# Input 0's load split anew between the instruction rings and the casting ring, and dummy matmuls counted from when TensorE wakes

## The chip, the cores and the metric

The kernel runs on one core of one Trainium2 chip. The metric is device time in microseconds (us), the median of several runs. Before the change it was 435.29 us (435.23 to 435.62, 4 runs). Engine names follow the profile: PE is TensorE, PEld its weight loads, DVE is VectorE, ACT is ScalarE, POOL is GpSimd, SP is SyncE. "The casting ring" is the DMA queue that POOL feeds; in this kernel it turns fp32 into fp16 on the way. "The instruction rings" are the queues that SP and ACT feed; in this kernel they copy without a cast. In the traces, each group of input 0 that comes by them has a cast of its own on ACT or DVE (0.43 to 0.62 us each, L456), and the groups of the casting ring have none.

## The reference, cut to what matters

For each of 8 batches: a real Fourier transform along 2496 rows, a complex 256 x 256 mix with bias and soft threshold, the inverse transform, and then a mixture-of-experts layer in which each batch goes through one expert.

```
X = rfft(x, axis=1)                        # x: (8, 2496, 256) fp32
Yr = Xr @ w_r - Xi @ w_i + b_r             # and Yi alike
Y = soft_threshold(Yr) + 1j * soft_threshold(Yi)
y = irfft(Y)
e = argmax(mean(y, axis=1) @ w_gate)       # one expert per batch
out = gate * (relu(y @ w1[e]) @ w2[e])
```

Nothing can start before input 0 (batch 0 of x) is in SBUF. It has 11 column groups of 117 partitions x 512 values. The first DFT (L657) turns them into spectra, the mix (L701) multiplies by the weights, a second DFT with the tables `tf` and `tm` (L734, L737) finishes the transform, and VectorE adds the bias (z, L749) and thresholds (L762, L764). Then come the inverse (L576, L615, L1000) and the experts (L1302, L1339). The first DFT of batch 1 (L657 again, from input 1) is done between the inverse products of batch 0.

## The kernel before: the parts that matter

A list scheduler written in Python fixes the order of every engine's instructions when the kernel is built. It keeps a clock of its own: `free[e]` is the time at which engine e is assumed free, and `S.fixed(t)` is an assumed landing time of a load. These numbers only decide the order; when things run is read from the traces (in the changed kernel the copy of a table part assumed at 16.4 us runs when the part comes, at 18.81). Dummy matmuls fill assumed idle time of PE, to keep its clock up: with dummies in an early wait they come 0.22 us apart after 11 us (e8 below), without them 0.43 (e1). "Cold", "half speed" and a clock that "rises" are read from the spacings of matmuls.

```python
def run(self):
    free = dict.fromkeys(("PE", "ACT", "DVE", "SP", "POOL"), 1.3)
    free["ACT"], free["SP"], free["POOL"] = 4.0, 3.5, 6.0
    ...
XF = 4                                   # groups 0..3: instruction rings, fp32
X0_CUTS = ((4, 8), (8, 11))              # groups 4..10: casting ring, fp16
...
x0_part(nc.sync, 0, 0, 2, xf); x0_part(nc.scalar, 2, 0, 2, xf); ...
x0_part(nc.scalar, 2, 2, 4, xf); x0_part(nc.sync, 0, 2, 4, xf); ...
for c0, c1 in X0_CUTS:
    for j in (0, 2, 1):
        x0_part(nc.gpsimd, j, c0, c1, xin0)
...
X0_AT, X1_AT = (5.0, 9.0, 11.5), 27.0    # assumed landings: input 0, input 1
W_AT, T_AT = 12.9, (13.8, 16.8, 19.0)    # weights; three parts of the tables
WARM, COLD, WARM_END = 60, 10, 13.2
...
for i in range(WARM):                    # dummies; a cold one is taken as 0.43 us
    o = S.op("PE", 0.43 if i < COLD else 0.216, dummy, 1e6 + i)
    o.until = WARM_END
...
def tm_part(k0, k9, t):                  # VectorE: tm is tf with halves swapped, one negated
    ...
    return S.op("DVE", 0.1 + 0.055 * (k9 - k0), emit, -39, deps=[S.fixed(t)])
...
def load_w(_):                           # a tiny copy on POOL waits for a casting cut
    nc.gpsimd.tensor_copy(out=wf[0:1, :, 0, 0:1], in_=xin0[0:1, 4:6, 0:1])
    ...                                  # then SP loads w_r, w_i
def load_tables(_):                      # SP, behind the weights: tf, bias2, ti, in three parts
    ...
def load_1(_):                           # input 1, held behind tf's second part
    xin_t[1] = load_now(1, (0, NG // 2), tf[96:97, 11, 0:2])
```

So a chain of loads hangs together: a casting cut of input 0 lands, POOL makes a tiny copy (1 x 2 elements), SP issues weights and tables one after another, the second part of `tf` lands, POOL makes another tiny copy, and input 1 is issued on the casting ring. In the schedules below, "the gate" is the first of these copies.

Of the kernel before, what the change touches and what calls it, by code (L numbers as in the profile page):

```python
# [135 lines left out]
class Schedule:  # L136
# [59 lines left out]

    def run(self):
        free = dict.fromkeys(("PE", "ACT", "DVE", "SP", "POOL"), 1.3)
        free["ACT"], free["SP"], free["POOL"] = 4.0, 3.5, 6.0
        ring = {"SP": 19.0, "POOL": 25.5}  # L200
        todo = sorted(self.ops, key=lambda o: o.vt)
        self.log = []
        while any(not o.until for o in todo):
            best = None
            seen = {e: 0 for e in free}
            for o in todo:
                if all(seen[e] > 24 for e in o.engs):
                    continue
                r = self.ready(o)
                if r is None or (o.until and max(r, free["PE"]) > o.until):  # L210
                    continue
                for e in o.engs:
                    seen[e] += 1
                    s = max(r, free[e])
                    p = o.bias if s < RAMP else 0.0
                    if e == "DVE" and len(o.engs) > 1:
                        p += o.pen
                    if o.until:
                        p += IDLE
                    k = (s + p, o.vt, s + p + o.lat[e])  # L220
                    if best is None or k < best[0]:
                        best = (k, s, o, e)
            _, s, o, e = best
            todo.remove(o)
            for k in o.allocs:
                if k.tag in self.rings:
                    self.bank[k.tag] = self.rings[k.tag].take(k)
                else:
                    self.hist.setdefault(k.tag, []).append(k)
            free[e] = s + o.occ[e]  # L230
            o.done = s + o.lat[e]
            if o.dma:
                other = "POOL" if e == "SP" else "SP"
                t = max(ring[e], s + 1.3)
                behind = max(0.0, ring[other] - t)
                if e == "SP":
                    ext = min(2.3 * o.dma, behind)
                    ring[other] += ext / 2.3
                else:
                    ext = min(0.43 * o.dma, behind)  # L240
                    ring[other] += min(2.3 * behind, o.dma)
                ring[e] = t + o.dma + ext
                o.done = ring[e] + o.slack
            self.log.append((s, e, o))
            o.emit(e)
# [3 lines left out]
def kernel(  # L249
# [12 lines left out]
    nc = tc.nc  # L262
# [9 lines left out]
        return ctx.enter_context(tc.tile_pool(name=name, bufs=bufs, **kw))  # L272

    XROW = 2 * D + 16
    XF = 4
    X0_CUTS = ((4, 8), (8, 11))
    BUFS = {"XT": 2, "hs": 2, "z": 3, "V": 3, "Pt": 2}
    cpool = pool("consts", 1)
    xpool = pool("xp", 2)
# [18 lines left out]
    def load_now(b, cuts, hold=None):  # L298

        xin = xpool.tile([117, NG // 2, XROW], FP16, name="xin")  # L300
        if hold is not None:
            nc.gpsimd.tensor_copy(out=xin[96:97, 0, 0:2], in_=hold)
        xv = x[b].rearrange("(a n) c -> a n c", n=N2)
        for c0, c1 in zip(cuts, cuts[1:]):
            for j in range(3):
                nc.gpsimd.dma_start(
                    out=xin[39 * j : 39 * j + 39, c0:c1, 0 : 2 * D],
                    in_=xv[:, 21 * j + 2 * c0 : 21 * j + 2 * c1, :].rearrange(
                        "a (g i) c -> a g (i c)", i=2))
        return xin  # L310
# [5 lines left out]
    xin0 = xpool.tile([117, NG // 2, XROW], FP16, name="xin")  # L316
    xf = hpool.tile([117, XF, 2 * D], FP32, name="hs")
    xv = x[0].rearrange("(a n) c -> a n c", n=N2)

    def x0_part(eng, j, c0, c1, dst):  # L320
        eng.dma_start(
            out=dst[39 * j : 39 * j + 39, c0:c1, 0 : 2 * D],
            in_=xv[:, 21 * j + 2 * c0 : 21 * j + 2 * c1, :].rearrange(
                "a (g i) c -> a g (i c)", i=2))
# [2 lines left out]
    x0_part(nc.scalar, 2, 0, 2, xf)  # L327
    x0_part(nc.sync, 1, 0, 2, xf)
    nc.scalar.dma_start(out=wa, in_=d_wa.ap())
    x0_part(nc.scalar, 2, 2, 4, xf)  # L330
    x0_part(nc.sync, 0, 2, 4, xf)
    x0_part(nc.sync, 1, 2, 4, xf)
    for c0, c1 in X0_CUTS:
        for j in (0, 2, 1):
            x0_part(nc.gpsimd, j, c0, c1, xin0)
# [8 lines left out]
    for e in range(E):  # L344
        nc.vector.memset(iot[:, e : e + 1], float(E - e))
    wf = ypool.tile([P, N], FP32, name="ysb")[:, 0 : 4 * D].rearrange(
        "p (w t c) -> p w t c", w=2, t=2)
# [12 lines left out]
    KT = ((0, 4), (4, 12), (12, 20))  # L360
# [4 lines left out]
    wg16 = cpool.tile([P, 2, E], FP16, name="wg16")  # L365


    X0_AT, X1_AT = (5.0, 9.0, 11.5), 27.0
    W_AT, T_AT = 12.9, (13.8, 16.8, 19.0)



    S = Schedule(BANKS)
# [3 lines left out]
    DIRECT = 2  # L377
    WIDE1 = 1
    W_LATE = 46.0
    WARM, COLD, WARM_END = 60, 10, 13.2  # L380
    LATE = -0.12
    FAST = {(B - 1, c) for c in range(4)}
    PERIOD, SPAN, SHIFT = 49.5, 1.4, 0.6
# [18 lines left out]
    def tm_part(k0, k9, t):  # L402
        def emit(_):
            nc.vector.tensor_scalar_mul(out=tm[:, k0:k9, 0:64],
                                        in0=tf[:, k0:k9, 64:P], scalar1=-1.0)
            nc.vector.tensor_copy(out=tm[:, k0:k9, 64:P], in_=tf[:, k0:k9, 0:64])
        return S.op("DVE", 0.1 + 0.055 * (k9 - k0), emit, -39, deps=[S.fixed(t)])

    tm_in = {k: o for (k0, k9), t in zip(KT, T_AT)
             for o in [tm_part(k0, k9, t)] for k in range(k0, k9)}  # L410

    def w_products(_):
# [9 lines left out]
        for i, bv in enumerate((b_r, b_i)):  # L422
            nc.sync.dma_start(out=bias[:, i], in_=spread(bv, P))
    S.op("SP", 0.8, bias_load, W_LATE, deps=[S.fixed(W_LATE)])
    b_in = S.fixed(T_AT[0])
    yk = S.tok("ysb", 2)
    yk.rel.append(w_late)
    S.preset(yk)
# [3 lines left out]
        nc.sync.dma_start(out=wi0, in_=d_wi0.ap())  # L432
        nc.sync.dma_start(out=wi, in_=d_wi.ap())
    S.op("SP", 1.8, small_loads, -30, deps=[S.fixed(13.0)], lat=8.0)
    small = S.fixed(18.0)


    pw = ps[:, BASE["o"]]
    for i in range(WARM):
        def dummy(_):  # L440
            nc.tensor.matmul(pw, warm[:, 0:P], warm)  # L441
        o = S.op("PE", 0.43 if i < COLD else 0.216, dummy, 1e6 + i)
        o.until = WARM_END

    def wg_cast(eng):
        COPY[eng](out=wg16, in_=wg)
    wg_in = S.evac(20, wg_cast, 0.5, deps=[small])
    t_in = [S.fixed(T_AT[0 if k1 < 4 else 1 if k1 < 12 else 2])
            for k1 in range(NK1)]
    first_V2 = S.tok("V2", 2)  # L450
    S.preset(first_V2)
# [2 lines left out]
    def x_cast(c):  # L454
        def emit(eng):
            COPY[eng](out=xin0[:, c, 0 : 2 * D], in_=xf[:, c])  # L456
        return S.evac(500, emit, -60 + c, deps=[S.fixed(X0_AT[0] + 0.3 * c)])

    x_cast_ops = [x_cast(c) for c in range(XF)]
    c1, c2 = ([S.fixed(t)] for t in X0_AT[1:])  # L460
    xdone = {0: [x_cast_ops[0:2], x_cast_ops[2:4], c1, c1, c2, c2],
             1: [S.fixed(X1_AT)]}
    xin_t[0] = xin0

    def load_w(_):
        nc.gpsimd.tensor_copy(out=wf[0:1, :, 0, 0:1], in_=xin0[0:1, 4:6, 0:1])
        for i, w in enumerate((w_r, w_i)):
            nc.sync.dma_start(out=wf[:, i], in_=w.rearrange("(t p) c -> p t c", p=P))
    S.op("SP", 1.0, load_w, -80, deps=[S.fixed(7.0)])

    def load_tables(_):
# [11 lines left out]

    def load_1(_):
        xin_t[1] = load_now(1, (0, NG // 2), tf[96:97, 11, 0:2])
    S.op("POOL", 2.4, load_1, -78, deps=[S.fixed(14.5)])
    xtok = {b: S.tok("xin", 2) for b in range(B)}
    for b in range(2):
        S.preset(xtok[b])
# [947 lines left out]
```

## Time and profile before

| | before |
|---|---|
| time | 435.29 us |
| span of the profiled run | 434.1 us |
| PE wakes / first real matmul (L657) | 3.87 / 8.96 us |
| gate (POOL) | 9.67 us |
| mix (L701) starts | 16.78 us |
| second z on DVE (L749) | 20.84 us |
| first DFT of batch 1 | 32.34 us |
| first expert matmul (L1302) | 47.64 us |

The page of the kernel before gives the span, then the busy time of each engine with its share, and, in part 4, the chain of work that ended last.

```profile
span 434.1 us, 9428 instructions
PE 423.7 (98%) x3572; PEld 314.9 (73%) x3572; DVE 301.9 (70%) x616; ACT 332.7 (77%) x643; POOL 33.1 (8%) x54
PE 93%; DVE 3%; ACT 2%; issue 1%; ACTq 0%
```

PE bounds the kernel, but "busy" includes the dummies. The timeline of PE before shows them. The columns are start, duration, engine, line, operation, output<-input, size, how many in a row, and in brackets the idle time before and what ended it.

```profile
3.87 5.30 PE L441 MATMUL ps<-warm 128*128 128x512 f16 x12 [3.87 <-ACT warm L339]
8.96 1.53 PE L657 MATMUL ps<-wa,xin 117*128 117x120 f16 x16
10.33 2.11 PE L441 MATMUL ps<-warm 128*128 128x512 f16 x9
12.28 1.00 PE L657 MATMUL ps<-wa,xin 117*128 117x120 f16 x16
13.12 1.68 PE L441 MATMUL ps<-warm 128*128 128x512 f16 x7
14.63 0.73 PE L657 MATMUL ps<-wa,xin 117*128 117x120 f16 x12
15.21 1.46 PE L441 MATMUL ps<-warm 128*128 128x512 f16 x6
...
32.34 0.58 PE L657 MATMUL ps<-wa,xin 117*128 117x120 f16 x8
...
47.64 1.02 PE L1302 MATMUL ps<-ysb,w1s 128*128 128x512 f16 x4
```

No L657 up to 16 us has a bracket: PE never waits for data, its data waits behind dummies. PE wakes 2.6 us later than the 1.3 us that the scheduler assumed, so every dummy is that late.

### The profile page before, as it was taken

The page shows a single profiled execution, that of the slowest core. Times are in us where ns is not written, and L with a number is a line of the kernel's source. Part 1 is how long each engine was busy: PE and PEld are TensorE (multiplying, and loading weights), DVE is VectorE, ACT ScalarE, POOL GpSimd, SP SyncE. Part 2 cuts the span into 40 slices and gives each one's busy share as a digit, 9 for nine tenths or more (in the row PEclk, how much of TensorE's full clock was granted, in tenths as well). Part 3 has the DMA queues.
Part 4 walks back from the last instruction along what each step waited for, and adds up shares of the span by engine and source line. Part 5 has one row for each costly group of instructions (what it writes and reads, how often), then busy time and mean ns, then how long its engine had stood idle before and what let it go on. Part 6 is the DMA issues. An engine that isn't in the chain of part 4 may idle for free.

```text
span 434.1 us, 9428 instructions
## 1 busy us (share of the span) xinstructions
PE 423.7 (98%) x3572; PEld 314.9 (73%) x3572; DVE 301.9 (70%) x616; ACT 332.7 (77%) x643; POOL 33.1 (8%) x54
## 2 busy tenths in 40 slices
PE   6998999999999999999999999999999999999996
PEld 3557666778777877778677777778777787777775
DVE  1488866577967687786977878777877869513661
ACT  3589987688877787678867888768777788678884
POOL 3230100021002000021001100020000010000000
PEclk9999999999999999999999999999999999999999
DMA  8899197989994998879986998959977276522122
GB/s 166 223 160 171 33 228 227 215 160 189 231 277 121 226 188 227 241 151 217 189 236 206 189 204 207 292 96 233 207 211 227 101 140 148 173 91 74 50 99 92
DMA packets 85605, 77.20 MB, mean 178 GB/s; under 512 B 7610, under 2 KB 72398, under 8 KB 85560
## 3 DMA queue, kind: packets, MB, share of 16 engines
q1 hardware_dynamic: 68366, 57.73, 47.7%
q0 software_dynamic: 16880, 18.46, 27.7%
q8 instruction: 28, 0.46, 0.4%
q10 hardware_dynamic: 314, 0.41, 0.3%
q14 instruction: 17, 0.14, 0.1%
HBM read 57.54 MB, written 37.49 MB: 219 GB/s over the span
## 4 chain that ended last, share of the span: by engine, by line
PE 93%; DVE 3%; ACT 2%; issue 1%; ACTq 0%
PE ps L1302 31%; PE ps L1339 29%; PE ps L897 9%; PE ps L1042 4%; PE ps L529 4%; PE ps L795 3%; PE ps L859 3%; PE ps L701 3%; PE ps L1221 2%; PE ps L441 2%; DVE z L749 1%; PE ps L734 1%; PE ps L657 1%; PE ps L737 1%; DVE Y L764 1%
## 5 line engine op out<-in xcount | busy, mean ns | idle before, releaser
L1314 ACT ACTIVATE hs<-ps 128x512 f16<-128x512 f32 (+1 forms) x293 | 168.2, 594 | 68.1 <-PE ps L1302 64.3
L1302 PE MATMUL ps<-ysb,w1s 128*128 128x512 f16 (+1 forms) x640 | 178.2, 374 | 0.0
L1339 PE MATMUL ps<-w2s,hs 128*128 128x256 f16 x1152 | 162.3, 272 | 0.1
L1339 PEld LDWEIGHTS <-hs 128*128 128x128 f16 x1152 | 110.8, 98 | 42.7 <-issue 0.2
L1302 PEld LDWEIGHTS <-w1s 128*128 128x128 f16 x640 | 68.6, 113 | 18.6 <-issue 0.2
L911 DVE TENSOR_TENSOR tt<-ps,bias 128x512 f16<-128x512 f32 x60 | 38.6, 686 | 24.5 <-PE ps L897 24.5
L939 DVE TENSOR_TENSOR Y<-z,cl 64x512 f16<-64x512 f16 x120 | 50.4, 420 | 2.8
L897 PE MATMUL ps<-w,XT 128*128 128x256 f16 x360 | 49.4, 273 | 0.0
L1356 ACT ACTIVATE ost<-ps,gbc 128x512 f32<-128x512 f32 x65 | 44.8, 689 | 2.3 <-PE ps L1339 2.3
L897 PEld LDWEIGHTS <-XT 128*128 128x128 f16 x360 | 35.2, 98 | 7.7
L920 DVE TENSOR_TENSOR z<-ps,tt 128x512 f16<-128x512 f32 x60 | 38.4, 681 | 0.1
L805 ACT CAST A<-ps 120x512 f16<-120x512 f32 x48 | 29.4, 613 | 7.2 <-PE ps L795 6.8
L1058 DVE CAST ysb<-ps 128x468 f16<-128x468 f32 (+1 forms) x24 | 15.0, 630 | 25.6 <-PE ps L1042 25.5
L1058 ACT CAST ysb<-ps 128x468 f16<-128x468 f32 (+1 forms) x60 | 28.0, 522 | 3.2 <-PE ps L1042 2.6
L867 DVE CAST XT<-ps 128x512 f16<-128x512 f32 x24 | 16.5, 688 | 16.0 <-PE ps L859 16.0
L536 ACT CAST V<-ps 128x512 f16<-128x512 f32 x45 | 26.1, 607 | 0.0
L795 PE MATMUL ps<-xin,wa 117*120 117x512 f16 x66 | 23.1, 380 | 0.4 <-ACT ysb L1015 0.4
L1042 PE MATMUL ps<-wi,V 120*128 120x117 f16 (+1 forms) x308 | 22.4, 214 | 0.0
L867 ACT CAST XT<-ps 128x512 f16<-128x512 f32 x36 | 22.0, 614 | 0.0
L529 PE MATMUL ps<-Y,ti 128*128 128x256 f16 x140 | 21.8, 272 | 0.0
L536 DVE CAST V<-ps 128x512 f16<-128x512 f32 x25 | 17.2, 688 | 6.4 <-PE ps L529 5.4
L1042 PEld LDWEIGHTS <-V 120*128 120x128 f16 x308 | 19.8, 98 | 2.4
(104 smaller groups left out, 421.6 us busy)
## 6 DMA issues: line engine op xcount, KB each, us to landing
out_dram<-ost SPq DMA_DIRECT2D x72, 256.0 KB
xin<-in_x_dram POOLq DMA_DIRECT2D x21, 429.0 KB, 11.0
scr<-V SPq DMA_DIRECT2D x35, 256.0 KB
XB<-fwd SPq DMA_DIRECT2D x30, 256.0 KB
V<-scr SPq DMA_DIRECT2D x14, 504.0 KB
fwd<-A SPq DMA_DIRECT2D x18, 360.0 KB
w1s<-in_moe_w_dram POOLq DMA_DIRECT2D x8, 512.0 KB, 7.3
w2s<-in_moe_w_dram POOLq DMA_DIRECT2D x8, 512.0 KB, 8.8
```

The source lines that it names most:

```text
L529: nc.tensor.matmul(pv[:, D * i : D * i + D], ti[:, 4 * q + k, :], cell["Y"](k))
L536: COPY[eng](out=hc["V"][:, n * u : n * u + n].rearrange("p i c -> p (i c)"), in_=hc["p", u])
L867: COPY[eng](out=cell["X"][:, ch, :, 0:2].rearrange("p a r i k -> p a i r k"), in_=hc["p"].rearrange("p (a i r k) -> p a i r k", a=2, i=2, ...
L897: nc.tensor.matmul(pm[:, D * a : D * a + D], cell["X"][:, ch, a, t].rearrange("p i k -> p (i k)"), w4[:, ch, t, :], start=(ch == 0), stop= ...
L911: nc.vector.tensor_add(out=cell["tt"][:, r], in0=cell["T", 2].rearrange("p (a c) -> p a c", a=2), in1=bias[:, r].unsqueeze(1).to_broadcast ...
L939: nc.vector.tensor_sub(out=Y[64 * r : 64 * r + 64, :, i], in0=cell["z"][s, r], in1=cell["cl"][s, r])
L1042: nc.tensor.matmul(pi[:, 117 * i : 117 * i + M], V2[:, g, ch * P : ch * P + P], w)
L1058: COPY[eng](out=yv[:, :, 12 * gb : 12 * gb + 3 * nf].rearrange("p a (g j) -> p a g j", j=3), in_=pi[:, 0 : 117 * nf].rearrange("p (g a j) ...
L1302: nc.tensor.matmul(ph[:, 0:nl], w1v[:, ch, fc // 4, :, fc % 4], ysb_t[b][:, ch, ns : ns + nl], start=(ch == 0), stop=(ch == 1))
L1314: nc.scalar.activation(out=o, in_=i, func=AFT.Relu)
L1339: nc.tensor.matmul(oc["p"][:, i, :], cell["hs"][:, ft, s0 : s0 + P], w2s_t[b][:, ft, :], start=(ft == 0), stop=(ft == E - 1))
L1356: nc.scalar.activation(out=ost, in_=oc["p"], func=AFT.Copy, scale=gbc_t[b])
```

## The change

Its intent is to start the real work as early as the data allows. Only groups 0 and 1 stay on the instruction rings. The casting ring takes nine groups in three cuts. PE's dummies are counted from 3.85 us, and the assumed landings are all moved earlier to suit.

```diff
-        free["ACT"], free["SP"], free["POOL"] = 4.0, 3.5, 6.0
-        ring = {"SP": 19.0, "POOL": 25.5}
+        free["PE"], free["ACT"], free["SP"], free["POOL"] = 3.85, 4.0, 3.5, 6.0
+        ring = {"SP": 17.5, "POOL": 26.0}
@@
-    XF = 4
-    X0_CUTS = ((4, 8), (8, 11))
+    XF = 2
+    X0_CUTS = ((2, 6), (6, 9), (9, 11))
@@
-    x0_part(nc.scalar, 2, 2, 4, xf)
-    x0_part(nc.sync, 0, 2, 4, xf)
-    x0_part(nc.sync, 1, 2, 4, xf)
@@
-    X0_AT, X1_AT = (5.0, 9.0, 11.5), 27.0
-    W_AT, T_AT = 12.9, (13.8, 16.8, 19.0)
+    X0_AT, X1_AT = (5.2, 7.6, 9.4, 10.8), 26.5
+    W_AT = 11.6
+    TF_AT, TI_AT = (12.3, 14.4, 16.4), (13.2, 15.4, 17.4)
@@
-    WARM, COLD, WARM_END = 60, 10, 13.2
+    WARM, COLD, WARM_END = 60, 12, 11.9
@@ (load_w's gate now reads the second of the three cuts)
-        nc.gpsimd.tensor_copy(out=wf[0:1, :, 0, 0:1], in_=xin0[0:1, 4:6, 0:1])
+        nc.gpsimd.tensor_copy(out=wf[0:1, :, 0, 0:1], in_=xin0[0:1, 6:8, 0:1])
... (the uses of these constants, and smaller assumed times, cut)
```

Lines of the changed kernel are two below those of before: L657 becomes L655, L701 becomes L699, L749 becomes L747, L1302 becomes L1300. Experiments on the kernel before keep its lines; in e10 and e11 the lines after the table loads are one below those of before (L749 becomes L748).

More of the change, by code (lines that the diff above doesn't have):

```diff
@@ L407, in tm_part @@
         return S.op("DVE", 0.1 + 0.055 * (k9 - k0), emit, -39, deps=[S.fixed(t)])
-    tm_in = {k: o for (k0, k9), t in zip(KT, T_AT)
+    tm_in = {k: o for (k0, k9), t in zip(KT, TF_AT)
              for o in [tm_part(k0, k9, t)] for k in range(k0, k9)}
@@ L424 @@
     S.op("SP", 0.8, bias_load, W_LATE, deps=[S.fixed(W_LATE)])
-    b_in = S.fixed(T_AT[0])
+    b_in = S.fixed(13.0)
     yk = S.tok("ysb", 2)
@@ L434 @@
     S.op("SP", 1.8, small_loads, -30, deps=[S.fixed(13.0)], lat=8.0)
-    small = S.fixed(18.0)
+    small = S.fixed(16.5)
     pw = ps[:, BASE["o"]]
@@ L447 @@
     wg_in = S.evac(20, wg_cast, 0.5, deps=[small])
-    t_in = [S.fixed(T_AT[0 if k1 < 4 else 1 if k1 < 12 else 2])
+    t_in = [S.fixed(TI_AT[0 if k1 < 4 else 1 if k1 < 12 else 2])
             for k1 in range(NK1)]
@@ L456, in emit @@
             COPY[eng](out=xin0[:, c, 0 : 2 * D], in_=xf[:, c])
-        return S.evac(500, emit, -60 + c, deps=[S.fixed(X0_AT[0] + 0.3 * c)])
+        return S.evac(500, emit, -60 + c, deps=[S.fixed(X0_AT[0])])
     x_cast_ops = [x_cast(c) for c in range(XF)]
-    c1, c2 = ([S.fixed(t)] for t in X0_AT[1:])
-    xdone = {0: [x_cast_ops[0:2], x_cast_ops[2:4], c1, c1, c2, c2],
+    c1, c2, c3 = ([S.fixed(t)] for t in X0_AT[1:])
+    xdone = {0: [x_cast_ops, c1, c1, c2, c3, c3],
              1: [S.fixed(X1_AT)]}
@@ L485, in load_1 @@
         xin_t[1] = load_now(1, (0, NG // 2), tf[96:97, 11, 0:2])
-    S.op("POOL", 2.4, load_1, -78, deps=[S.fixed(14.5)])
+    S.op("POOL", 2.4, load_1, -78, deps=[S.fixed(13.5)])
     xtok = {b: S.tok("xin", 2) for b in range(B)}
```

## The prediction

> **What bounds the kernel.** The page shows TensorE (PE) busy 98% of a 434.1 us span and holding 93% of the chain that ended last; the table of stretches shows it at 100% from 50 to 400 us. So time saved before the first expert matmul (L1302, 47.6 us) can reach the end one for one; the rest of the program changes only in order.
>
> **The start, from the timeline.** PE wakes at 3.87 us, but the schedule counts dummies from 1.3 us, so it emits twelve cold ones of 427 ns (3.87 to about 9.0). The first two column groups were cast by 6.4 us (casts 5.23 to 6.37), yet the first DFT matmul (L657) starts at 8.96, behind dummies. It repeats: nine dummies from 10.33, seven from 13.12, six from 15.21. PE never waits for a load here; its queue is about 2.6 us late. The chain runs dummies, L657, dummies, L657, dummies, L657, weight cast, then L701 at 16.78.
>
> **Loads.** Groups 2 and 3 on the instruction rings landed only at 9.33 us. The DMA view gives about 8.2 us from issue to landing for the casting transfers, so the first cut landed between 9.7 and 11.3 us, the second at 12 to 13. The DMA engines are 96% busy or more from 4 to 10 us, so moving two groups to another ring removes no work, only competition: [...] the casting queue moved 386 packets in 5 to 8 us beside the instruction rings, 497 in 8 to 10 us alone. From those rates I estimate that the three new cuts land near 7.8, 9.6 and 11.2 us. Weight loads now wait for the first part of the second cut, near 8.4 us instead of 9.67; the tables behind them come 1 to 1.5 us earlier.
>
> **What changes.** Two casts of 0.43 to 0.62 us go. POOL issues nine transfers of 0.63 us instead of six, until about 7.2 us; off the chain. About five dummies precede the first L657, near 6.0 us. The last L657 group starts near 11.2 instead of 14.6, its eviction (0.96 us) ends near 12.6, weights are cast by 12.4, and L701 starts near 13.0 instead of 16.78.
>
> **What reaches the end.** 3.7 us is freed at L701. Tables and input 1 come only 1 to 2 us earlier (input 1 landed near 30 us, first used at 32.34), and the 17 to 47 us stage alternates between PE, ACT and DVE; I estimate 0.7 us lost there. Expected: **432.3 us**, 80% range **430.9 to 434.4**. Chances: faster by over 2% 0.01, within 2% 0.97, slower by over 2% 0.02.
>
> **What would show it.** Right: first L657 near 6 us; fewer dummies before L701; gate copy on POOL near 8.4; L701 near 13; first L1302 at 44 to 45; PE still 100% from 50 us. Wrong: L657 waits for loads; L701 waits for the weight cast; PE idle near 28 us for input 1; matmuls turning cold in gaps.
>
> **What would make it wrong.** The re-drawn order could open later PE gaps of a microsecond; casting transfers could serialise, the last landing after 12.5 us; or 17 to 47 us may be bound by DVE or tables, so that the gain is given back by 47 us.

## More of the kernel before

DVE before, from the weight cast on, with the three parts of the table copy (L404):

```profile
15.81 0.42 DVE L397 CAST w<-ysb 128x512 f16<-128x512 f32 x1
16.14 0.22 DVE L404 TENSOR_SCALAR V<-tf 128x256 f16<-128x256 f16 x1
...
19.54 0.69 DVE L749 TENSOR_TENSOR z<-ps,bias 128x512 f16<-128x512 f32 x1 [3.04 <-PE ps L737]
20.15 0.28 DVE L404 TENSOR_SCALAR V<-tf 128x512 f16<-128x512 f16 x1
...
20.84 0.69 DVE L749 TENSOR_TENSOR z<-ps,bias 128x512 f16<-128x512 f32 x1 [0.21 <-PE ps L737]
...
22.63 0.68 DVE L749 TENSOR_TENSOR z<-ps,bias 128x512 f16<-128x512 f32 x1
23.23 0.28 DVE L404 TENSOR_SCALAR V<-tf 128x512 f16<-128x512 f16 x1
```

None of the table copies waits for its load here: DVE gets to them so late that the tables are there. Note the order: the third copy (23.23) comes after the third z (22.63).

## The result, and the profile after

The changed kernel took 434.11 us (433.95 to 434.79, 4 runs), against 435.29. A ratio in this document is the mean time of one kernel's fast runs over the mean of the other's of the same rounds, so it is not quite the ratio of the medians quoted. Here it is 0.9974, 95% interval 0.9957 to 0.9991. That is inside the predicted range, but the gain is 1.2 us where 3.0 were expected.

The page of the kernel after, with the same parts:

```profile
span 433.1 us, 9390 instructions
PE 419.6 (97%) x3553; PEld 312.2 (72%) x3553; DVE 300.8 (69%) x614; ACT 333.0 (77%) x643; POOL 35.4 (8%) x57
PE 89%; DMA 5%; ACT 3%; POOL 1%; SPq 1%; issue 0%; DVE 0%; ACTq 0%; POOLq 0%
```

DMA, absent from the chain before, now holds 5% of it. PE's timeline after:

```profile
3.45 2.31 PE L439 MATMUL ps<-warm 128*128 128x512 f16 x5 [3.45 <-ACT warm L336]
6.04 0.98 PE L655 MATMUL ps<-wa,xin 117*128 117x120 f16 x8 [0.28 <-ACT xin L454]
...
8.47 1.00 PE L655 MATMUL ps<-wa,xin 117*128 117x120 f16 x16 [0.67 <-DMA xin<-in_x_dram]
...
13.76 1.89 PE L699 MATMUL ps<-w,XB 128*128 128x512 f16 x8 [1.04 <-ACT w L395]
...
31.04 0.58 PE L655 MATMUL ps<-wa,xin 117*128 117x120 f16 x8 [0.32 <-DMA xin<-in_x_dram]
...
46.31 1.02 PE L1300 MATMUL ps<-ysb,w1s 128*128 128x512 f16 x4
```

Real work now waits for data instead of for dummies, and the mix starts 3.02 us earlier (16.78 - 13.76). But the first DFT of batch 1 is only 1.30 us earlier (32.34 - 31.04), and so is the first expert matmul (47.64 - 46.31 = 1.33). Between 14 and 31 us, 1.7 us are given back. DVE after shows one place:

```profile
15.75 0.29 DVE L402 TENSOR_SCALAR V<-tf 128x512 f16<-128x512 f16 x1 [1.77 <-DMA tf<-d_tf]
...
16.52 0.69 DVE L747 TENSOR_TENSOR z<-ps,bias 128x512 f16<-128x512 f32 x1 [0.28 <-PE ps L735]
18.81 0.29 DVE L402 TENSOR_SCALAR V<-tf 128x512 f16<-128x512 f16 x1 [1.59 <-DMA tf<-d_tf]
...
19.22 0.68 DVE L747 TENSOR_TENSOR z<-ps,bias 128x512 f16<-128x512 f32 x1
```

The third table copy now stands in DVE's queue in front of the second z; before the change it stood behind the third z. So the new assumed times moved it. Its part of `tf` was assumed at 16.4 us and came at 18.8. The matmul for the second z was over by 17.8 (the last L735 of that pair starts at 17.51 and takes 0.27), yet z starts at 19.22. That z is 1.62 us earlier than before (20.84 - 19.22), not 3.02. DVE did not take it ahead of the table copy: there are 1.59 us of waiting at the head of the queue, during the last 1.0 us of which the z behind it was ready.

The other suspect is input 1. The chain that ended last, after, in order of time (start, length, what):

```profile
3.44 5.62 DMA xin<-in_x_dram
9.12 0.19 POOL ysb L464
...
12.68 3.05 DMA tf<-d_tf
15.78 0.31 POOL xin L302
...
17.51 13.39 DMA xin<-in_x_dram
...
31.04 0.59 PE ps L655 x8
```

This is the chain of loads described above. Input 1's last part is issued at 17.51 and lands at 30.90 us. By the same reckoning (issue plus the DMA view's time to landing) it landed at 30.60 before: the gate came only 0.55 us earlier, and what it set off was no faster.

### The profile page after: what moved, and what is told of

Its sections match the earlier page's. It is cut to its first block, busy times and chain, and to the rows that moved or that the text cites. A ratio compares the mean times of both kernels' runs of the same rounds, so it can differ in the third digit from the quotient of the medians.

```text
span 433.1 us, 9390 instructions
## 1 busy us (share of the span) xinstructions
PE 419.6 (97%) x3553; PEld 312.2 (72%) x3553; DVE 300.8 (69%) x614; ACT 333.0 (77%) x643; POOL 35.4 (8%) x57
## 4 chain that ended last, share of the span: by engine, by line
PE 89%; DMA 5%; ACT 3%; POOL 1%; SPq 1%; issue 0%; DVE 0%; ACTq 0%; POOLq 0%
PE ps L1300 30%; PE ps L1337 29%; PE ps L895 9%; DMA xin<-in_x_dram 4%; PE ps L1040 4%; PE ps L527 3%; PE ps L793 3%; PE ps L857 3%; PE ps L1219 2%; PE ps L699 2%; ACT hs L1312 1%; DMA tf<-d_tf 1%; PE ps L613 1%; PE ps L732 0%; POOL xin L321 0%
## 5 line engine op out<-in xcount | busy, mean ns | idle before, releaser
L1300 PE MATMUL ps<-ysb,w1s 128*128 128x512 f16 (+1 forms) x640 | 178.4, 374 | 0.1
L1300 PEld LDWEIGHTS <-w1s 128*128 128x128 f16 x640 | 68.6, 113 | 18.8 <-issue 0.6
L803 ACT CAST A<-ps 120x512 f16<-120x512 f32 x48 | 29.5, 614 | 7.0 <-PE ps L793 6.6
## 6 DMA issues: line engine op xcount, KB each, us to landing
xin<-in_x_dram POOLq DMA_DIRECT2D x21, 429.0 KB, 11.3
```

The source lines that it names most:

```text
L1300: nc.tensor.matmul(ph[:, 0:nl], w1v[:, ch, fc // 4, :, fc % 4], ysb_t[b][:, ch, ns : ns + nl], start=(ch == 0), stop=(ch == 1))
```

## The experiments

Twelve kernels were run on three chips, four at a time, each group beside runs of the kernel before. The rival explanations were: (A) DVE's queue blocked on the forward table; (B) input 1's landing; (C) the re-drawn order of instructions; (D) a split that gives nothing, all the gain coming from the dummies. Milestones are from each one's own trace; "in 1 lands" is issue plus time to landing, from the DMA view.

| run | time | before beside it | ratio (95%) | mix | 2nd z | in 1 lands | DFT b1 | 1st expert |
|---|---|---|---|---|---|---|---|---|
| before | 435.29 | | | 16.78 | 20.84 | 30.60 | 32.34 | 47.64 |
| after | 434.11 | 435.29 | 0.9974 (0.9957-0.9991) | 13.76 | 19.22 | 30.90 | 31.04 | 46.31 |
| r_after | 434.86 | 435.60 | 0.9990 (0.9977-1.0004) | 15.09 | 19.35 | 30.57 | 30.70 | 46.33 |
| e1_count_only | 436.42 | 435.55 | 1.0011 (0.9998-1.0024) | 18.00 | 22.06 | 32.03 | 33.56 | 48.87 |
| e2_split_only | 435.26 | 435.55 | 0.9998 (0.9986-1.0010) | 15.70 | 19.76 | 30.11 | 31.27 | 46.91 |
| e3_tm_late | 435.12 | 435.55 | 0.9999 (0.9982-1.0016) | 13.84 | 17.90 | 33.14 | 33.27 | 49.29 |
| e4_bias_late | 434.23 | 435.55 | 0.9977 (0.9965-0.9989) | 13.53 | 18.40 | 28.75 | 29.74 | 45.38 |
| e5_hold_w1 | 440.55 | 435.60 | 1.0107 (1.0093-1.0122) | 13.72 | 18.62 | 30.81 | 30.94 | 50.68 |
| e6_tm_bias | 433.85 | 435.60 | 0.9962 (0.9950-0.9975) | 13.78 | 17.84 | 28.16 | 29.34 | 44.98 |
| e7_tm_bias_hold | 438.40 | 435.60 | 1.0073 (1.0053-1.0093) | 14.04 | 18.10 | 28.87 | 29.60 | 48.13 |
| e8_count_landing | 434.58 | 435.38 | 0.9982 (0.9969-0.9995) | 15.13 | 19.20 | 30.89 | 30.98 | 46.16 |
| e9_landings | 435.62 | 435.38 | 0.9994 (0.9978-1.0009) | 15.05 | 20.39 | 29.98 | 31.90 | 47.36 |
| e10_tf_first | 434.00 | 435.38 | 0.9966 (0.9953-0.9979) | 13.80 | 17.86 | 30.65 | 30.78 | 46.06 |
| e11_tf_first_bias | 433.90 | 435.38 | 0.9968 (0.9955-0.9980) | 13.61 | 17.66 | 27.97 | 29.18 | 44.83 |

One trace is one run, and runs of one kernel differ by up to a microsecond or more, so the times and intervals decide and the traces explain. The first trace of the changed kernel is of its slowest run (434.79, median 434.11), that of e10 too (434.54), and those of e6 and e11 are of their fastest (433.42 and 433.53). So traces differ by more than the medians do.

### The two halves of the change apart

e1_count_only: the kernel before with the dummies counted anew and nothing else.

```diff
-        free["ACT"], free["SP"], free["POOL"] = 4.0, 3.5, 6.0
+        free["PE"], free["ACT"], free["SP"], free["POOL"] = 3.85, 4.0, 3.5, 6.0
-    WARM, COLD, WARM_END = 60, 10, 13.2
+    WARM, COLD, WARM_END = 60, 12, 13.2
```

> The kernel before with only the dummies counted from 3.85 us and twelve of them taken as cold; the column split and all landing guesses stay as before. Theory (the queue of dummies is the late start, and what follows is limited by loads): first L657 near 6 us instead of 8.96; but groups 2 and 3 still land at 9.3 us and the second casting cut near 12.9 us, so L701 starts near 14.5 to 15 us (before 16.78, changed kernel 13.76). If input 1 then decides (its load hangs behind the same gate at 9.67 us, so it lands near 30 to 31 us), the total falls by 0.3 to 1.0 us, to 434.3 to 435.0. Rival (the split is what helps, the dummies only fill idle time): total within 0.2 us of 435.29.

Both theories missed: it was not faster at all (436.42 beside 435.55, interval touching 1). The first DFT did start at 5.97, but its timeline then shows a hole:

```profile
5.97 1.13 PE L657 MATMUL ps<-wa,xin 117*128 117x120 f16 x8
9.72 0.98 PE L657 MATMUL ps<-wa,xin 117*128 117x120 f16 x8 [2.61 <-DVE xin L456]
10.49 2.34 PE L441 MATMUL ps<-warm 128*128 128x512 f16 x5
12.62 1.81 PE L657 MATMUL ps<-wa,xin 117*128 117x120 f16 x16
14.22 1.79 PE L441 MATMUL ps<-warm 128*128 128x512 f16 x4
```

Groups 2 and 3 were assumed at about 5.6 us and landed at 9.23, so no dummies stood in that wait. The clock stayed at half speed: five dummies then span 2.34 us (0.43 each), where in the kernel before nine took 2.11 (0.22 apart). The late dummies before had hidden a wrong landing time.

e8_count_landing is e1 with that one landing time corrected.

```diff
-        return S.evac(500, emit, -60 + c, deps=[S.fixed(X0_AT[0] + 0.3 * c)])
+        return S.evac(500, emit, -60 + c, deps=[S.fixed(X0_AT[0] + 0.3 * c if c < 2 else 9.2)])
```

> The run e1 (old split, dummies counted from 3.85 us) was slower than before (436.42 against 435.55): groups 2 and 3 were assumed at 5.6 us, so TensorE had no dummies and stood idle from 7.1 to 9.72 us; after that its dummies took 427 ns each up to 15.5 us, and L701 started at 18.0. Here the casts of groups 2 and 3 are assumed at 9.2 us, their measured landing, so dummies fill that wait; nothing else differs from e1. Theory (the idle stretch sent the clock back to half speed and the dummies emitted for a warm clock then took double): dummies after 10.5 us take 216 ns, L701 starts at 14.3 to 15.5 us, 2.5 us or more earlier than in e1, and the total is 0.3 us or more below e1's. Rival (the loads of the old split are what held e1): L701 stays after 17 us.

```profile
7.14 2.40 PE L441 MATMUL ps<-warm 128*128 128x512 f16 x8
10.40 1.03 PE L657 MATMUL ps<-wa,xin 117*128 117x120 f16 x16 [0.86 <-ACT xin L456]
11.26 1.03 PE L441 MATMUL ps<-warm 128*128 128x512 f16 x4
```

The theory holds, except that the clock in e1 did not fall in the wait: it had not risen yet (the L657 from 5.97 us are 0.10 us apart, those from 15.85 us 0.05). Four dummies after 11 us span 1.03 us (0.22 apart), the mix starts at 15.13, 2.87 us before e1's, and the time is 434.58: 0.9982 of before, with the old split. (The scheduler re-draws the order of PE, DVE and ACT with the new number; that the clock rose is shown by the spacing of the dummies.) So the count with a true landing time gives about what the whole change gives (0.9974 and 0.9990 in its two sets).

e2_split_only: the changed kernel with the dummies counted as before.

```diff
-        free["PE"], free["ACT"], free["SP"], free["POOL"] = 3.85, 4.0, 3.5, 6.0
+        free["ACT"], free["SP"], free["POOL"] = 4.0, 3.5, 6.0
-    WARM, COLD, WARM_END = 60, 12, 11.9
+    WARM, COLD, WARM_END = 60, 10, 11.9
```

> The changed kernel with the dummies again counted from 1.3 us and ten taken as cold; the split and its landing guesses stay. Theory: the casting cuts land as in the changed kernel (8.5, 10.1, 11.4 us), but the first L655 waits behind 9 to 12 cold dummies until 8 to 9 us and L699 starts at 15 to 16 us; total between 434.3 and 435.2. Rival (the split brings the gain): total within 0.2 us of the changed kernel's 434.1.

It came out just past the slow end of the range: 435.26, 0.9998 of before. The casting cuts land as in the changed kernel (the last at 11.4), the first L655 starts at 8.11 and the mix at 15.70. The split brings nothing measurable without the count. What it does in the full change is remove the late landing of groups 2 and 3, the one that hurt e1.

### The forward table, and the order of instructions

e3_tm_late moves only the assumed landings of `tf`'s second and third part, so that the table copies stand later in DVE's queue.

```diff
-    TF_AT, TI_AT = (12.3, 14.4, 16.4), (13.2, 15.4, 17.4)
+    TF_AT, TI_AT = (12.3, 16.6, 20.0), (13.2, 15.4, 17.4)
```

> The changed kernel with only the assumed landing of the forward table's second and third part moved from 14.4 and 16.4 to 16.6 and 20.0 us, so that VectorE's in-order queue has the sign-flipped copies of these tables after the additions that already have their data. Theory A (VectorE blocked on a table until 18.8 us and pushed the second z from 17.8 to 19.22 us; after that input 1, landing at 30.9 us, decides): the second z starts near 17.8, the first inverse matmul L574 at 19.8 to 20.2 instead of 21.21, but L655 of batch 1 still starts at 30.9 or later, and the total gains 0 to 0.3 us, 433.8 to 434.1. Theory B (the blocked VectorE alone costs the gain): L655 of batch 1 near 29.5 us and total 432.6 to 433.0. Theory C (re-drawn order, neither): no milestone moves by over 0.3 us.

The first half of theory A holds: the second z starts at 17.90, the first inverse at 20.36 instead of 21.21. The rest was worse than expected: the total, 435.12, is no better than before the change. Input 1 landed at 33.14 in this trace and PE stood 3.71 us before batch 1's DFT:

```profile
33.27 0.58 PE L655 MATMUL ps<-wa,xin 117*128 117x120 f16 x8 [3.71 <-DMA xin<-in_x_dram]
```

The profiled run was one of two long ones (437.74 and 437.48); the other four took 434.83 to 435.28. So lifting the table alone runs into the limit on input 1. Why it landed 2 us later here is not known.

e10_tf_first is the clean test: it changes only the order in which SP issues the tables, all of `tf` before `ti`. The orders of PE, DVE, ACT and POOL were compared with the changed kernel's and are identical.

```diff
     for k0, k9 in KT:
         nc.sync.dma_start(out=tf[:, k0:k9], in_=d_tf.ap()[:, k0:k9])
         ... (bias2, wg)
-        nc.sync.dma_start(out=ti[:, k0:k9], in_=d_ti.ap()[:, k0:k9])
+    for k0, k9 in KT:
+        nc.sync.dma_start(out=ti[:, k0:k9], in_=d_ti.ap()[:, k0:k9])
```

> The changed kernel with only the order of its table loads changed: all three parts of the forward table before the inverse table. The order of every compute instruction is exactly the changed kernel's. Theory A (VectorE's queue stands blocked on the forward table): its second part lands 0.5 us and its third about 1 us earlier, so the second z starts near 18.0 to 18.4 instead of 19.2, the first inverse near 20.3 instead of 21.2, the first DFT of batch 1 near 29.9 to 30.3, and the total falls by 0.4 to 1.0 us. Theory C (what was lost was lost by the re-drawn order, not by the tables): no change of the total beyond 0.2 us.

```profile
17.16 0.29 DVE L402 TENSOR_SCALAR V<-tf 128x512 f16<-128x512 f16 x1
...
17.86 0.69 DVE L748 TENSOR_TENSOR z<-ps,bias 128x512 f16<-128x512 f32 x1 [0.20 <-PE ps L736]
...
30.78 0.58 PE L656 MATMUL ps<-wa,xin 117*128 117x120 f16 x8 [1.24 <-DMA xin<-in_x_dram]
```

The third table copy no longer waits, and the second z starts at 17.86, 1.36 us earlier than in the changed kernel, now waiting for PE. The first inverse is at 20.31. Batch 1's DFT gains only 0.26 us (31.04 - 30.78), less than expected, because it now waits 1.24 us for input 1, which landed at 30.65. The time, 434.00, is 0.9966 of before. Its interval overlaps those of the changed kernel, so the total alone would not prove it. But with the order unchanged, the 1.36 us at the second z come from the table's earlier landing. The order has its part all the same: e3 left the table's load as it was, moved its copy back behind (20.43), and lifted the same block (second z at 17.90). The re-drawn order and the late table block DVE together; mending either is enough for that z.

r_after, the changed kernel again, was sent to see how far input 1's landing varies.

> The changed kernel once more, unedited, beside the three below. Its first trace was of its slowest run (434.79 us, median 434.11). Theory (input 1's landing decides and varies from run to run): in this trace input 1 lands at another time than 30.90 us, and L655 of batch 1 and the span move with it by the same amount as long as it lands after 30.7 us. Rival (the landing does not matter): L655 of batch 1 at 31.0 wherever input 1 lands. Total 433.9 to 434.5.

It told something else. In this trace the cuts land 0.2 to 0.4 us later, the clock stays cold longer (three dummies from 6.97 span 1.48 us, against 0.98 from 6.82), and the mix starts at 15.09, 1.33 us later than in the first trace. Yet its second z starts at 19.35, only 0.13 later:

```profile
18.94 0.29 DVE L402 TENSOR_SCALAR V<-tf 128x512 f16<-128x512 f16 x1 [0.40 <-DMA tf<-d_tf]
...
19.35 0.68 DVE L747 TENSOR_TENSOR z<-ps,bias 128x512 f16<-128x512 f32 x1
```

From the start of the mix to the second z it is 4.06 us where nothing blocks (before, e10), 5.46 in the first trace and 4.26 here. So the table cost 1.40 us in the first trace and 0.20 here, where the late mix had used up the rest. Input 1 landed 0.33 us earlier (30.57) and its DFT began 0.34 earlier (30.70), but the first expert matmul (46.33 against 46.31) and the span (433.2 against 433.1) did not move with it. The total, 434.86, missed its range too, and its ratio of 0.9990 is not apart from 1. The late mix is not the rule: in the eight other traces with this first stage (after, e3 to e7, e10, e11) the mix starts between 13.53 and 14.04.

### Input 1

e4_bias_late issues two broadcast loads of `bias`, which only batch 2 needs, near 50 us instead of right behind the tables. PE's order is identical to the changed kernel's.

```diff
-    S.op("SP", 0.8, bias_load, W_LATE, deps=[S.fixed(W_LATE)])
+    S.op("SP", 0.8, bias_load, 54.0, deps=[S.fixed(54.0)])
```

> The changed kernel with the two broadcast loads of bias (128 KB each, needed only by batch 2) issued near 50 us instead of at 16.5 to 17.4 us, where they share the DMA engines with the load of input 1 until 24 us. Theory (input 1's landing decides, and its load is slowed by what runs beside it): input 1 lands at 29.5 to 30.4 us instead of 30.90, the wait of 0.32 us at L655 of batch 1 goes, and the total falls by 0.2 to 0.5 us. Rival (input 1 is not the limit): total within 0.1 us of 434.1 and L655 of batch 1 at 31.0.

The DMA view of 19 to 24 us, by queue (packets, MB, share of the 16 engines' time), of the changed kernel and then of this run:

```profile
q0 software_dynamic: 716, 0.58, 77.0%
q1 hardware_dynamic: 279, 0.24, 22.8%
```

```profile
q0 software_dynamic: 990, 0.85, 115.2%
```

The casting ring moves 0.85 MB instead of 0.58 in the same 5 us, and input 1 lands at 28.75 (29.5 to 30.4 were expected) instead of 30.90. The other traces agree: from the first issue of input 1 to its last landing it is 12.2 to 13.6 us in the five with the bias late (e4, e6, e7, e9, e11) and 14.0 to 16.8 in the nine others. No wait is left before batch 1's DFT, which starts at 29.74. Part of this gain is not input 1's: the third table copy runs at 17.99 instead of 18.81 and the second z at 18.40. In this trace that is 0.8 us, more than the 0.3 us of waiting for input 1. The time is 434.23, 0.9977 of before, which is not apart from the changed kernel's two values.

e5_hold_w1 holds back batch 0's expert weights, which follow input 1 on the casting ring, until input 1 has landed.

```diff
             w1s = wpool.tile([P, 2, F], FP16, name="w1s")
+            if b == 0:
+                nc.gpsimd.tensor_copy(out=w1s[64:65, 0, 0:2], in_=xin_t[1][96:97, 10, 0:2])
```

> The changed kernel, but the expert weights of batch 0 (w1s, w2s; issued at 26.2 us behind input 1 on the same casting ring) wait, by a one-element copy that reads the last landed part of input 1, until input 1 is there. Theory (the weights, issued 1.7 us earlier than before the change, take DMA engines from input 1's tail, which moves only about 100 KB/us from 27 to 31 us): input 1 lands 1 us or more earlier, at 28.5 to 30 us, L655 of batch 1 does not wait, total 0.2 to 0.6 us below the changed kernel beside it; unless input 2, now later, makes L793 wait near 45.5 us. Rival (the tail is slow by itself): input 1 still lands at 30.5 to 31.5 us and the total stays or grows.

The theory fell. Input 1 landed at 30.81, 14.85 us after its first issue (14.87 in the changed kernel), as if nothing had been taken away. And the side effect came true: input 2, behind these weights, was late, and PE stood for 4.33 us at its first use.

```profile
49.35 0.68 PE L793 MATMUL ps<-xin,wa 117*120 117x512 f16 x1 [4.33 <-DMA xin<-in_x_dram]
```

The time rose to 440.55. e7_tm_bias_hold adds the same hold to e6 below.

> The former with batch 0's expert weights held behind input 1 as well. Theory (the weights slow input 1's tail): input 1 lands 0.5 to 1.5 us earlier than in the former, near 28 us, L655 of batch 1 at 28.7 to 29.0 us, total 0 to 0.6 us below the former. If input 2 becomes late instead, L793 of batch 2 waits for it near 44 us and the total is above the former. Rival: input 1 lands as in the former.

Again input 1 was hardly faster (12.22 us from first issue to landing, at 28.87, against 12.34, at 28.16, without the hold), and PE waited 3.31 us for input 2: 438.40. In neither trace do the expert weights slow input 1's tail.

### Both limits at once

e6_tm_bias has the edits of e3 and e4 together.

> The changed kernel with both edits that each move one limit: the table copies later on VectorE (alone 435.12: the first inverse 0.85 us earlier, but input 1 landed at 33.1 us) and the bias broadcasts late (alone 434.23: input 1 at 28.75 us, L655 of batch 1 at 29.74). Theory (two limits stand behind each other: tables on VectorE, then input 1): together the first inverse at 19.5 to 20.0 us, input 1 lands at 28.5 to 29.5 us and L655 of batch 1 starts at 28.8 to 29.6; total 0.5 to 1.2 us below the changed kernel beside it. Rival (something else bounds 14 to 31 us): L655 of batch 1 stays at 29.7 or later and the total within 0.3 us of the changed kernel.

The theory holds: second z 17.84, input 1 at 28.16, batch 1's DFT at 29.34, first expert matmul at 44.98. The time is 433.85 beside 434.86 for the changed kernel and 435.60 for the one before, ratio 0.9962. This version beats both on the same chip: its interval ends at 0.9975, the changed kernel's begins at 0.9977. The first inverse, at 20.29, was later than the 19.5 to 20.0 expected.

e11_tf_first_bias has the edits of e10 and e4 together.

> The former with the bias broadcasts late as well; again the order of every compute instruction is the changed kernel's. Theory A with input 1 behind it: third part of the forward table lands near 17 us, input 1 near 27.5 to 28.5, second z at 17.8 to 18.2, first DFT of batch 1 at 29.2 to 29.6 us; total 1.0 to 1.6 us below the changed kernel's and near that of the best so far (0.9962 of before). If the total stays within 0.3 us of the former, the bias broadcasts cost nothing by themselves once the tables are early.

```profile
29.18 0.59 PE L656 MATMUL ps<-wa,xin 117*128 117x120 f16 x8
```

Second z 17.66, input 1 at 27.97, batch 1's DFT at 29.18 without a wait, first expert matmul at 44.83, earlier than in all other traces. With both limits lifted nothing is lost any more between the mix and batch 1's DFT: against the kernel before, the mix is 3.17 us earlier and that DFT 3.16 (e6: 3.00 and 3.00). The time, 433.90, ratio 0.9968, equals e6's within the intervals, and equals e10's too. So in the total the two ways of unblocking DVE agree, and what the late bias adds on top of early tables is not shown by the times (434.00 and 433.90); the 1.60 us between e10 and e11 at batch 1's DFT are those of one trace each.

e9_landings is e6 with the assumed landings of input 0 and the weights set to the measured ones.

```diff
-    X0_AT, X1_AT = (5.2, 7.6, 9.4, 10.8), 26.5
-    W_AT = 11.6
+    X0_AT, X1_AT = (5.4, 8.4, 10.0, 11.4), 26.5
+    W_AT = 12.3
-    WARM, COLD, WARM_END = 60, 12, 11.9
+    WARM, COLD, WARM_END = 60, 12, 12.4
```

> The best so far (table copies later, bias late: 433.85 beside 434.86 for the changed kernel) with the assumed landings of input 0 and of the weights set to those measured (5.4, 8.4, 10.0, 11.4; weights 12.3) and dummies until 12.4. In the changed kernel L699 waited 1.0 us for the second weight cast, which ScalarE had queued behind two evictions. If the re-drawn order puts that cast earlier, L699 starts near 13.2 instead of 13.78 and the total falls by 0.2 to 0.5 us to 433.3 to 433.7; if VectorE's new order (table copy before the weight cast) holds it up, L699 is at 13.8 or later and the total is 433.8 or more.

It went the second way, and for the same reason as the change itself. The table's first part was still assumed at 12.3, so its copy was now put in front of the weight cast on DVE:

```profile
13.81 0.23 DVE L402 TENSOR_SCALAR V<-tf 128x256 f16<-128x256 f16 x1 [2.73 <-DMA tf<-d_tf]
...
14.49 0.42 DVE L395 CAST w<-ysb 128x512 f16<-128x512 f32 x1
```

PE waited 2.24 us for that cast and started the mix at 15.05. Six runs took 434.25 to 436.10. Correcting some of the assumed times and not others moved the fault to another instruction.

## Why the prediction was right or wrong

- **PE bounds the kernel, and time saved early reaches the end: right.** First expert matmul 1.33 us earlier; the last block of expert matmuls starts at 425.67 instead of 426.77, 1.10 us earlier; 1.18 us in the median time. In 13 of the 14 traces 386.4 to 387.1 us pass from the first expert matmul to the end of the span (388.2 in e5), so what is gained there stays gained to within 0.7 us.
- **The dummies' queue is 2.6 us late, first L657 near 6.0: right** (6.04). PE also woke at 3.45 instead of 3.87, because ACT issues one load less (0.39 us) before its table load, which starts at 1.90 instead of 2.32; the copy that PE waits for starts at 3.20 instead of 3.62. That was not foreseen, and it makes the new 3.85 too late again by 0.4 us.
- **Landings near 7.8, 9.6 and 11.2: nearly right.** The waits and the DMA view give about 8.3, 10.0 and 11.3. The first casting cut sped up when the instruction rings had less to move (three loads of 156 KB instead of six): 4.6 to 5.5 us from issue to landing instead of about 8.2, with 695 packets of the casting queue from 5 to 8 us instead of 386. That did not make it matter: e8 has the old split and is as fast.
- **Gate near 8.4, tables 1 to 1.5 us earlier: wrong.** The gate came at 9.12 (0.55 us earlier) and the second part of `tf` let input 1 go at 15.78 instead of 16.46 (0.68 us). In the other traces with this first stage the gate came between 8.53 and 9.51.
- **Weights cast by 12.4, mix near 13.0: the cast was late.** ACT had the second cast behind two evictions, from 13.08 to 13.71, and the mix started at 13.76. That is 3.0 us freed instead of 3.7.
- **"Tables and input 1 come only 1 to 2 us earlier ... I estimate 0.7 us lost there": this is the step that failed.** From 14 to 31 us, 1.72 us were lost (3.02 at the mix, 1.30 at batch 1's DFT). Input 1 came 0.30 us later, not earlier (30.90 against 30.60), and its wait ended last (0.32 us). Just behind stood DVE's queue, blocked until 18.8 us by a table assumed at 16.4, which held the second z 1.40 us. The two overlap and do not add up: e10 lifts the table alone and gains 0.26 us at batch 1's DFT; e6 and e11 lift both and lose nothing. The prediction named tables, input 1 and DVE as the risk, but priced it as a small friction, and did not ask which DVE instruction stands in front of which.
- **The sum.** Predicted 3.7 - 0.7 = 3.0 us; in the first trace 3.02 - 1.72 = 1.30. Of the 1.7 us missing, 0.7 fell at the late weight cast and 1.0 at the step above. That is the account of one trace: in the second the mix gained only 1.69 us (the clock rose later), nearly nothing was lost behind it, and the first expert matmul came at the same time.
- **"The re-drawn order could open later PE gaps": right in part.** The new order moved the third table copy from behind the third z to before the second, where it met a late table. The order alone is not the cause: e10 keeps it and recovers the 1.36 us at the second z. Nor is the table's landing alone: e3 leaves its load as it was and recovers 1.32.
- **Matmuls turning cold in gaps: in e9** (L732 and L735 behind the wait of 2.24 us are 0.21 us apart instead of 0.11). In e1 and in the changed kernel's second trace the clock did not fall but rose late (e1: dummies 0.43 us apart up to 15.5 us; second trace: the 16 L655 from 8.88 us span 1.76 us instead of 1.00); in the latter that cost nothing at the first expert matmul (46.33 against 46.31).

Left open: why input 1 landed at 33.14 us in e3, what makes input 1's tail slow, why the median times of e10 and e11 hardly differ where their traces do, and how much of the 1.0 us between e6 and the changed kernel belongs to each of its two edits.

## What to carry to other kernels

When a change frees an engine early, follow the queue of the next engine instruction by instruction and compare each assumed landing with the measured one: here one whose load came 2.4 us late (18.8 instead of 16.4) held a z that was ready at 17.8 until 19.22. Warm-up work that runs too late can hide wrong landing times (in e1 groups 2 and 3, assumed at 5.6 us, landed at 9.23), so move both together or neither. And ask of a gain at the first stage what the slowest chain of loads behind it lets through: here that chain moved by 0.6 us (gate 0.55, second part of `tf` 0.68) while the mix moved by 3.02, and 1.30 was left at the first DFT of batch 1.

## What the traces show of PE's clock and of the loads

- In e9 PE's matmuls became slow after a wait of 2.24 us. The dummies before it were 0.22 us apart. The eight mix matmuls after it spanned 2.71 us instead of 1.89 (changed kernel, after a wait of 1.04 us), and the L732 and L735 from 17.55 us were 0.21 us apart instead of 0.11, at a granted clock of 0.66 from 15 to 18 us.
- The changed kernel's dummies became fast at 7.2 us, 3.8 us after waking (the first of the three from 6.82 us took 554 ns, the next 379). Before the change twelve dummies from 3.87 to 8.96 us were all slow, over 5 us, and L657 until about 9.8 us (0.10 us apart, then 0.05). In e1, PE was still slow at 15.5 us, nearly 6 us after its wait ended at 9.72. The granted clock of these profiles does not show this first cold stretch: it reads 1.00 from 3 us on in the kernel before and in e1, and only the spacing of matmuls tells. A later fall, as in e9, does show.
- For the 1.32 MB of input 1, counted as it lands, the three casting transfers took 14.9 us from first issue (16.03) to last landing (30.90), and 13.0 us (15.77 to 28.75) in e4 with less beside them.
- The two loads of `bias`, of 128 KB each, repeat one row over all partitions. They held 22.8% of the DMA engines' time from 19 to 24 us, and without them (e4) the casting ring moved 0.85 MB instead of 0.58.
